# A windowed attention with a ReLU-gated FFN: k and q read row-major and put in order by the PSUM reads, casting loads on the Pool queue, and block 0's denominators in pairs on the ACT queue

## The chip, the cores and the metric

The kernel runs on one core of a Trainium2 chip. The metric is the device time of one execution in microseconds (us). Two runs of the kernel before gave 388.25 and 390.06 us, a median of 389.15 us. The profile is of one further execution.

The engines are named as in the profile: PE is TensorE (matmuls; PEld its weight loads), DVE is VectorE, ACT is ScalarE, POOL is GpSimd, SP is SyncE, which here only issues DMAs. ACT and POOL issue DMAs as well, in their own instruction order; only POOL's can change the data type on the way.

## The reference

Four batches (blocks), eight heads, 768 positions, head size 64; every query sees the first 4 positions (the sink) and the last 128. The attention's output, 3072 tokens of 512, goes through a gated FFN.

```python
scores = scale * np.matmul(q, k.transpose(0, 1, 3, 2))
keep = (pos[None, :] < n_sink) | ((rel >= 0) & (rel < window))      # 4 and 128
scores = np.where(keep, scores, -1000000000.0)
a = np.exp(scores - np.max(scores, axis=-1, keepdims=True))
a = a / (np.sum(a, axis=-1, keepdims=True) + 1e-09)
x = (a @ v) as 3072 x 512
out = (np.maximum(x @ w_gate, 0.0) * (x @ w_val)) @ w_out           # 512 -> 1536 -> 512
```

## The kernel before

Attention is done in units of one block and one pair of heads (`Unit`). Keys are taken in seven windows j of 128 rows, which step by 124; in each window's first four rows stands the sink. A full unit (blocks 1 to 3, twelve of them, `FU`) covers all 768 queries. Block 0 is cut at query 376 (`QCUT`) into four first halves `P0` (windows 0 to 2) and four second halves `P1` (windows 2 to 6), so that the FFN can begin on block 0's first half. Units use two sets of buffers in turn (`s`).

A unit's steps are: `load`, f32 rows of k, q and v by DMA into kf, qf and vf (k and v window by window, 124 rows apart; q row-major, each partition holding n rows in succession); `cast` to bf16 into kn, qn and vn, with copies of the sink rows into windows 1, 3 and 5; `T`, PE transposes of q (L145) and k (L148) into one PSUM tile `tps`, from which DVE copies two halves into qz (L153, L156: the queries, head by head, written in the order of the positions, so with a step of n elements) and ACT copies kT (L154); `S`, score matmuls (L164), the exp on ACT (L167) and the mask product on DVE (L168); `V`, the matmul with v and with a column of ones (L176), which also gives the denominators, copied to oab by ACT (L179).

`norm` takes the denominators through DRAM, since they are to be spread over partitions: row 64 of oab is written to den_tmp (L290), read back as dc (L269), inverted on DVE (L273), written to rcp_tmp (L274), and read as R, broadcast over 64 partitions (L279); then DVE multiplies oab and R into xT (L287). Every step is issued one `tick` after the one before. All of these DMAs stand on SP's queue, as do all loads but the first halves' v.

The FFN runs in chunks (`chunk`): four gate matmuls (L301), the ReLU on ACT (L304), four value matmuls (L307), the product on DVE (L309). There are 96 chunks, 12 for each half block. The output matmuls (L320) of a finished half block are spread between the next chunks.

The order on every engine is that of the program (`manual_schedule`). First the P0 units run by themselves (the prologue), then the stages of P1 and FU are laid between the chunks: two stages to a chunk for the first 18 chunks, then one. A full unit has six stages: T; V of the unit before, with the cast of the next; S of three groups; V of its own first part. Loads are issued three units ahead, casts (on POOL) one unit ahead. The FFN's weights come in by POOL's DMAs, which cast (`load_w`, L184, and `load_wo`, L188).

Of the kernel before, what the change touches and what calls it, by code (L numbers as in the profile page):

```python
# [9 lines left out]
F32 = mybir.dt.float32  # L10
# [11 lines left out]
def kernel(  # L22
# [36 lines left out]
    kf = [const.tile([128, 7, 2, 64], F32, name=f"kf{i}") for i in range(2)]  # L59
    vf = [const.tile([128, 7, 2, 64], F32, name=f"vf{i}") for i in range(2)]  # L60
    qf = [const.tile([128, 6, 2, 64], F32, name=f"qf{i}") for i in range(2)]
    kn = [const.tile([128, 7, 2, 64], BF16, name=f"kn{i}") for i in range(2)]
    vn = [const.tile([128, 7, 2, 128], BF16, name=f"vn{i}") for i in range(2)]
    qn = [const.tile([128, 6, 2, 64], BF16, name=f"qn{i}") for i in range(2)]
    kT = [const.tile([128, 7, 128], BF16, name=f"kT{i}") for i in range(2)]
# [3 lines left out]
    sink = const.tile([4, 2, NP, 2, 64], BF16, name="sink")  # L69
# [5 lines left out]

    class Unit:


        def __init__(self, i, b, p, half):
            self.i, self.b, self.p, self.half, self.s = i, b, p, half, i % 2  # L80
            if half == 0:
                self.js, self.q0, self.n, self.qn, sub = (0, 1, 2), 0, QCUT, 3, p // 2
                self.jo, self.qo, self.zo = 3 * sub, 3 * sub, 384 * sub
                self.qrows, self.qp = 384, 128
            elif half == 1:
                self.js, self.q0, self.n, self.qn = (2, 3, 4, 5, 6), QCUT, S - QCUT, 4
                self.jo, self.qo, self.zo = 0, 0, 0
                self.qrows, self.qp = S - QCUT, 98
            else:
                self.js, self.q0, self.n, self.qn = tuple(range(7)), 0, S, 6  # L90
                self.jo, self.qo, self.zo = 0, 0, 0
                self.qrows, self.qp = S, 128
            self.j5 = [j for j in self.js if j < 6]
            self.a, self.e = self.jo + self.j5[0], self.jo + self.j5[-1] + 1


        def load(self, eng=None, veng=None):
            eng, veng = eng or nc.sync, veng or eng or nc.sync
            s, a, e = self.s, self.a, self.e
            for en, x, dst in ((eng, k, kf[s]), (eng, q, qf[s]), (veng, v, vf[s])):  # L100
                for h in range(2):
                    src = x[self.b, 2 * self.p + h]
                    if x is q:
                        r = src[self.q0:self.q0 + self.qrows, :].rearrange("(p n) d -> p n d", n=self.qn)
                        en.dma_start(out=dst[0:self.qp, self.qo:self.qo + self.qn, h, :], in_=r)
                        continue
                    r = bass.AP(src.tensor, src.offset + 124 * self.j5[0] * D,
                                [[D, 128], [124 * D, e - a], [1, D]])
                    en.dma_start(out=dst[:, a:e, h, :], in_=r)  # L109
                if x is not q and 6 in self.js:  # L110
                    en.dma_start(out=dst[0:24, 6, :, :],  # L111
                                 in_=x[self.b, 2 * self.p:2 * self.p + 2, 744:768, :].rearrange("h s d -> s h d"))


        def cast(self, what, eng):
            s, a, e = self.s, self.a, self.e
            cp = eng.tensor_copy
            if what == "q":
                cp(qn[s][0:self.qp, self.qo:self.qo + self.qn, :, :].rearrange("p j h d -> p (j h d)"),  # L119
                   qf[s][0:self.qp, self.qo:self.qo + self.qn, :, :].rearrange("p j h d -> p (j h d)"))  # L120
                return
            w = 0 if what == "k" else 1
            src, dst = (kf[s], kn[s]) if w == 0 else (vf[s], vn[s])
# [204 lines left out]
    with tc.manual_schedule():  # L328
# [5 lines left out]
        for u in P0:  # L334
            u.load(nc.sync, nc.scalar)
# [172 lines left out]
```

## Time and profile before

| | |
|---|---|
| runs, median | 389.15 us (388.25 to 390.06) |
| profiled execution | 390.11 us, span 388.4 us |
| mean granted PE clock | 0.946 |
| busy, share of the span | PE 70%, DVE 53%, ACT 36%, POOL 21% |
| first FFN matmul that has all of its inputs | 82 us |
| qz copies on DVE (L153, L156), all | 79.8 us of 207.7 us busy |
| DMA | 37.74 MB, 85692 of 96241 packets under 512 bytes |

Busy shares are averages over stages with different limits: the prologue to 82 us, in which PE is mostly idle, the attention units between the chunks to about 318 us, and chunks alone behind that.

### The profile page before, as it was taken

What the parts mean: (1) busy time and instruction counts of PE and PEld (TensorE: products, weight loads), DVE (VectorE), ACT (ScalarE), POOL (GpSimd) and SP (SyncE); (2) the same over time, 40 slices, a digit from 0 to 9 for tenths busy, and PEclk for the clock granted to TensorE, in tenths of its full rate; (3) what the DMA queues carried; (4) which work ended last, traced back from release to release, by engine and by line L of the source; (5) the groups of instructions that cost most, each with busy time, mean ns of one, the idle gap of its engine ahead of it and who ended that gap; (6) DMA issues with size and microseconds to landing.
All of it is one profiled execution on the core that took longest, in us unless ns stands there. A gap on an engine that the chain in (4) does not pass through costs nothing.

```text
span 388.4 us, 5029 instructions
## 1 busy us (share of the span) xinstructions
PE 272.5 (70%) x1760; PEld 163.6 (42%) x1760; DVE 207.7 (53%) x286; ACT 141.3 (36%) x225; POOL 83.2 (21%) x203
## 2 busy tenths in 40 slices
PE   0245230176384695687498989898988999999996
PEld 0122120045252453444255555454645555555552
DVE  5661230347877767861847575767667544222220
ACT  1233120126343543531353544445363533333331
POOL 6240531307424304311404040404010000000000
PEclk9999999999887878969599999999999999999999
DMA  9957199565684554408074747291211211110002
GB/s 178 146 112 125 37 177 196 121 157 117 131 157 102 124 125 94 119 27 166 1 138 95 137 101 137 59 191 33 68 29 43 71 43 53 39 44 29 27 34 103
DMA packets 96241, 37.74 MB, mean 97 GB/s; under 512 B 85692, under 2 KB 92364, under 8 KB 96216
## 3 DMA queue, kind: packets, MB, share of 16 engines
q1 hardware_dynamic: 87208, 31.91, 37.5%
q0 software_dynamic: 5808, 4.72, 8.0%
q10 hardware_dynamic: 3200, 0.79, 1.0%
q8 instruction: 14, 0.23, 0.3%
q14 instruction: 11, 0.09, 0.1%
HBM read 35.64 MB, written 6.49 MB: 108 GB/s over the span
## 4 chain that ended last, share of the span: by engine, by line
PE 48%; DVE 24%; DMA 11%; ACT 6%; issue 4%; SPq 4%; POOL 1%; DVEq 0%; ACTq 0%; POOLq 0%
PE vp L307 14%; PE op L320 13%; PE gp L301 12%; DVE qz L153 10%; DVE qz L156 8%; PE sps L164 6%; DMA kf<-in_k_dram 4%; ACT kT L154 3%; DMA R<-rcp_tmp 3%; DMA dc<-den_tmp 2%; DVE xT L287 2%; PE ops L176 2%; ACT ee L167 2%; SPq L109 2%; SPq L111 1%
## 5 line engine op out<-in xcount | busy, mean ns | idle before, releaser
L307 PE MATMUL vp<-xT,wv 128*128 128x384 bf16 (+2 forms) x384 | 83.2, 342 | 14.2 <-ACT gs L304 14.2
L301 PE MATMUL gp<-xT,wg 128*128 128x384 bf16 (+2 forms) x384 | 84.9, 346 | 5.9 <-DVE hT L309 4.1
L320 PE MATMUL op<-wo,hT 128*128 128x512 bf16 x288 | 77.3, 384 | 0.0
L309 DVE TENSOR_TENSOR hT<-gs,vp 128x384 bf16<-128x384 f32 (+2 forms) x96 | 51.2, 547 | 43.4 <-PE vp L307 42.4
L164 PE MATMUL sps<-qz,kT 128*128 128x251 bf16 (+5 forms) x232 | 35.3, 293 | 47.8 <-DVE qz L156 39.5
L167 ACT ACTIVATE ee<-sps 128x1006 bf16<-128x1006 f32 (+4 forms) x52 | 46.1, 900 | 53.2 <-PE sps L164 53.2
L304 ACT ACTIVATE gs<-gp 128x384 f32<-128x384 f32 (+2 forms) x96 | 47.2, 492 | 41.4 <-PE gp L301 40.9
L307 PEld LDWEIGHTS <-wv 128*128 128x128 bf16 x384 | 39.2, 102 | 47.6 <-issue 25.9
L168 DVE TENSOR_TENSOR ee<-ee,msk 128x1006 bf16<-128x1006 bf16 (+4 forms) x52 | 33.8, 651 | 39.4 <-ACT ee L167 38.8
L287 DVE TENSOR_TENSOR xT<-oab,R 64x768 bf16<-64x768 f32 (+2 forms) x40 | 33.2, 830 | 34.4 <-DMA R<-rcp_tmp 34.1
L128 POOL CAST vn<-vf 128x768 bf16<-128x768 f32 (+2 forms) x20 | 14.7, 732 | 165.8 <-PE ops L176 163.1
L154 ACT COPY kT<-tps 128x896 bf16<-128x896 bf16 (+2 forms) x20 | 15.6, 778 | 95.1 <-DVE qz L153 95.1
L164 PEld LDWEIGHTS <-kT 128*128 128x128 bf16 x232 | 23.0, 113 | 63.6 <-issue 31.9
L156 DVE COPY qz<-tps 64x768 bf16<-64x768 bf16 (+2 forms) x20 | 40.0, 2000 | 17.1 <-ACT kT L154 17.1
L301 PEld LDWEIGHTS <-wg 128*128 128x128 bf16 x384 | 37.3, 103 | 27.6 <-issue 7.9
L176 PE MATMUL ops<-ee,vn 128*128 128x248 bf16 (+6 forms) x256 | 28.6, 255 | 25.8 <-DVE ee L168 18.1
L153 DVE COPY qz<-tps 64x768 bf16<-64x768 bf16 (+2 forms) x20 | 39.8, 1990 | 7.3 <-PE tps L148 7.2
L320 PEld LDWEIGHTS <-hT 128*128 128x128 bf16 x288 | 28.5, 99 | 25.9 <-issue 1.2
L176 PEld LDWEIGHTS <-vn 128*128 128x128 bf16 x256 | 22.5, 103 | 35.0 <-issue 26.5
L179 ACT COPY oab<-ops 65x752 f32<-65x752 f32 (+1 forms) x32 | 25.4, 795 | 25.5 <-PE ops L176 25.3
L145 PE MATMUL tps<-ident,qn 128*128 128x128 bf16 (+1 forms) x100 | 9.8, 236 | 18.5 <-DVE qn L119 18.3
L324 ACT COPY ot<-op 128x512 f32<-128x512 f32 x24 | 14.1, 587 | 22.2 <-PE op L320 22.2
(47 smaller groups left out, 117.9 us busy)
## 6 DMA issues: line engine op xcount, KB each, us to landing
out_dram<-ot SPq DMA_DIRECT2D x24, 256.0 KB
kf<-in_k_dram SPq DMA_DIRECT2D x24, 192.0 KB
qf<-in_q_dram SPq DMA_DIRECT2D x24, 192.0 KB
vf<-in_v_dram SPq DMA_DIRECT2D x24, 192.0 KB
R<-rcp_tmp SPq DMA_DIRECT2D x12, 384.0 KB
wg<-in_moe_w_gate_dram POOLq DMA_DIRECT2D x4, 384.0 KB, 6.3
wv<-in_moe_w_val_dram POOLq DMA_DIRECT2D x4, 384.0 KB, 8.1
wo<-in_moe_w_out_dram POOLq DMA_DIRECT2D x3, 512.0 KB, 16.3
```

The lines of the kernel that those rows point to most:

```text
L153: nc.vector.tensor_copy(zq[0], po[0:64])
L156: nc.vector.tensor_copy(zq[1], po[64:128])
L164: nc.tensor.matmul(out=ps[:, h, c0:c1], lhsT=kT[s][:, self.jo + j, :], rhs=qz[s][:, h, self.zo + q0:self.zo + q0 + c1 - c0], start=True, s ...
L167: nc.scalar.activation(x, ps[:, :, lo:hi], Act.Exp, bias=0.0, scale=scale)
L168: nc.vector.tensor_tensor(x, x, msk[:, gi, :, lo:hi], op=Alu.mult)
L176: nc.tensor.matmul(out=ps[:, h, o0:o0 + c1 - c0], lhsT=vn[s][:, self.jo + j, h, :], rhs=ee[s][:, gi, h, c0:c1], start=i == 0, stop=i == le ...
L287: nc.vector.tensor_tensor(x[64 * h:64 * h + 64, p, q0:q0 + n], oab[0:64, h, q0:q0 + n], R[0][:, h, 0:n], op=Alu.mult)
L301: nc.tensor.matmul(out=gp[:, 0:n], lhsT=wg[:, ko, m * 128:(m + 1) * 128], rhs=x[:, ko, c0:c0 + n], start=ko == 0, stop=ko == KO - 1)
L304: nc.scalar.activation(gs[:, 0:n], gp[:, 0:n], Act.Relu, bias=0.0, scale=1.0)
L307: nc.tensor.matmul(out=vp[:, 0:n], lhsT=wv[:, ko, m * 128:(m + 1) * 128], rhs=x[:, ko, c0:c0 + n], start=ko == 0, stop=ko == KO - 1)
L309: nc.vector.tensor_tensor(hT[:, m, c0:c0 + n], gs[:, 0:n], vp[:, 0:n], op=Alu.mult)
L320: nc.tensor.matmul(out=op, lhsT=hTs[b][:, m, t * 128:(t + 1) * 128], rhs=wo[:, m, :], start=m == 0, stop=m == FM - 1)
```

## The change

*Row-major k.* k is loaded as q is: each partition holds n rows in succession, n being 3 for a first half, 5 for a second and 6 for a full unit. The transposes leave the positions out of order in PSUM. kT (now 872 columns in the order of positions, the last 104 zero) is written in order by an ACT copy that reads PSUM with a step; so are the two halves of qz by DVE, where before PSUM was read in order and qz written with a step. k and q have a PSUM tile each, `tk` and `tq`; the first halves take them from the pool of the FFN. Even windows are now slices of kT; for the odd ones DVE copies 124 columns and the four sink columns into kTs.

*Full units' loads.* They go by POOL's DMAs, which cast from f32 into kn, qn and vn, with no staging and no casts; they are issued in the stage in which the unit before that one ends, one unit ahead. POOL still copies the sink rows of v (`sinkv`).

*Block 0's first denominators.* Each unit writes its own row of den_tmp; the other steps of the chain are made for two units at a time. All of it is issued from ACT's queue. One of the three ticks of each P0 unit is gone.

*Order of the setup.* The buffers' memsets come first; the mask copies on DVE are put behind the first T, and the later masks behind P1's load. P1[3]'s load is issued with P1[2]'s, and `load_wo` behind P1[0]'s T.

```diff
-                    r = bass.AP(src.tensor, src.offset + 124 * self.j5[0] * D,
-                                [[D, 128], [124 * D, e - a], [1, D]])
-                    en.dma_start(out=dst[:, a:e, h, :], in_=r)
+        def load(self, eng, veng, staged):
+            for en, x, dst, r0, pp, nn in ((eng, k, kf[s] if staged else kn[s], self.kr, self.kp, self.kn),
+                                           (eng, q, qf[s] if staged else qn[s], self.qr, self.qp, self.qn)):
+                for h in range(2):
+                    en.dma_start(out=dst[0:pp, self.no:self.no + nn, h, :],
+                                 in_=x[b, 2 * p + h, r0:r0 + pp * nn, :].rearrange("(p n) d -> p n d", n=nn))
+            dst, o = (vf[s], self.vi) if staged else (vn[s], self.vo)
...
+        def sinkv(self, eng):
+            s, odd = self.s, [j for j in self.js if j % 2]
+            src = vn[s][0:4, self.vo, :, 0:64] if self.half != 1 else vsink[:, self.p, :, :]
+            eng.tensor_copy(vn[s][0:4, self.vo + odd[0]:self.vo + odd[-1] + 1:2, :, 0:64], bc(src, len(odd)))
...
-            zq = [qz[s][64 * h:64 * h + 64, h, z0:z0 + w].rearrange("d (p n) -> d n p", n=nq) for h in range(2)]
-            nc.vector.tensor_copy(zq[0], po[0:64])
-            nc.scalar.copy(kT[s][:, self.jo + d0:self.jo + d1, :].rearrange("p j n -> p (j n)"),
-                           ps[:, 1, d0 * 128:d1 * 128])
-            nc.vector.tensor_copy(zq[1], po[64:128])
+            ps = ptile("tk")
...
+            nc.scalar.copy(kT[s][:, k0:k0 + kp * kn_].rearrange("d (p n) -> d p n", n=kn_),
+                           ps[:, 0:kp * kn_].rearrange("d (n p) -> d p n", n=kn_))
+            pq = ptile("tq")
...
+            for h in range(2):
+                r = slice(64 * h, 64 * h + 64)
+                nc.vector.tensor_copy(qz[s][r, h, z0:z0 + qp * qn_].rearrange("d (p n) -> d p n", n=qn_),
+                                      pq[r, 0:qp * qn_].rearrange("d (n p) -> d p n", n=qn_))
+            odd = [j for j in self.js if j % 2]
+            i0, c0 = (odd[0] // 2 + self.no // 3), self.zo + 124 * odd[0] + 4
+            a = kT[s][:, c0:c0 + 124]
+            nc.vector.tensor_copy(kTs[s][:, i0:i0 + len(odd), 4:128],
+                                  bass.AP(a.tensor, a.offset, [a.ap[0], [248, len(odd)], [1, 124]]))
...
+            nc.vector.tensor_copy(kTs[s][:, i0:i0 + len(odd), 0:4], bc(src, len(odd)))
+
+        def kw(self, j):
+            if j % 2:
+                return kTs[self.s][:, j // 2 + self.no // 3, :]
+            c = self.zo + 124 * j
+            return kT[self.s][:, c:c + 128]
...
-    def norm(b, p, oab, q0, n, d):
+    def norm(b, ps, oabs, q0, n, d, eng, first=True, ticks=after):
...
+            eng.dma_start(out=dc[0:pp, 0:g, 0:cc], in_=view(den_d))
...
+            for p in ps:
+                R.append(rpool.tile([64, 2, S], F32, name="R"))
+                eng.dma_start(out=R[-1][:, :, 0:n],
+                              in_=rcp_d[b, p, 2 * q0:2 * (q0 + n)].rearrange("(h s) -> h s", h=2).partition_broadcast(64))
...
         def V0(p):
-            o = new_oab()
-            P0[p].V(0, o)
-            norm(0, p, o, 0, QCUT, 1)
+            o0.append(new_oab())
+            P0[p].V(0, o0[p])
+            den(0, p, o0[p], 0, QCUT, nc.scalar)
+            if p % 2:
+                norm(0, (p - 1, p), o0[p - 1:p + 1], 0, QCUT, 1, nc.scalar)
...
+        P0[0].T(*GV)
+        setup_m0()
...
             P0[p].S("G0")
-            tick()
             P0[p].S("G1a")
...
+                    nxt = at(x + 1)
+                    if nxt is not None:
+                        if nxt.half == 1:
+                            if x >= 1:
+                                casts(nxt)
+                        else:
+                            nxt.load(nc.gpsimd, nc.gpsimd, False)
```

Three places show how rows move. On DVE, the T of the first full unit, before:

```order
L153 COPY qz_99<-tps 64x6x128
L156 COPY qz_99<-tps 64x6x128
L287 TENSOR_TENSOR xT<-oab_105,R 64x392 x2
L273 RECIPROCAL dr<-dc 98x8
L309 TENSOR_TENSOR hT<-gs,vp 128x376
```

and in the change:

```order
L173 COPY qz_101<-tq 64x768 x2
L178 COPY kTs_99<-kT_97 128x3x124
L183 COPY kTs_99<-kT_97 128x3x4
L330 TENSOR_TENSOR xT<-oab_107,R 64x392 x2
L313 RECIPROCAL dr<-dc 98x8
L354 TENSOR_TENSOR hT<-gs,vp 128x376
```

Two copies have come in, the second and third row; the rest stands as it did.

On SP, the den chain of block 0's third and fourth unit (oab_106 and oab_103) and P1[2]'s load, before:

```order
L290 DMA den_tmp<-oab_106 2x1x376
L269 DMA dc<-den_tmp 94x8
L290 DMA den_tmp<-oab_103 2x1x376
L109 DMA kf_85<-in_k_dram 128x4x64 x2
L111 DMA kf_85<-in_k_dram 24x2x64
L105 DMA qf_89<-in_q_dram 98x4x64 x2
L109 DMA vf_87<-in_v_dram 128x4x64 x2
L111 DMA vf_87<-in_v_dram 24x2x64
L274 DMA rcp_tmp<-dr 94x8
L269 DMA dc<-den_tmp 94x8
L279 DMA R<-rcp_tmp 64x2x376
```

and the same chain in the change, on ACT (oab_108 and oab_105 are the third and fourth unit):

```order
L314 DMA rcp_tmp<-dr 94x2x8
L212 COPY oab_108<-ops 65x2x376
L335 DMA den_tmp<-oab_108 2x1x376
L320 DMA R<-rcp_tmp 64x2x376 x2
L212 COPY oab_105<-ops 65x2x376
L335 DMA den_tmp<-oab_105 2x1x376
L164 COPY kT_97<-tk 128x520
L309 DMA dc<-den_tmp 94x2x8
L200 ACTIVATE ee_103<-sps 128x2x375
L314 DMA rcp_tmp<-dr 94x2x8
L200 ACTIVATE ee_103<-sps 128x2x415
L320 DMA R<-rcp_tmp 64x2x376 x2
```

No load stands between the steps any more; what stands there is ACT's own work on P1[0] (kT_97 and ee_103).

On POOL, what a full unit has before:

```order
L125 CAST kn_91<-kf_85 128x768
L130 CAST kn_91<-kf_85 24x128
L135 CAST kn_91<-kf_85 4x128 x3
L119 CAST qn_95<-qf_89 128x768
L128 CAST vn_93<-vf_87 128x12x64
L130 CAST vn_93<-vf_87 24x2x64
L135 CAST vn_93<-vf_87 4x2x64 x3
```

and in the change:

```order
L116 DMA kn_91<-in_k_dram 128x6x64 x2
L116 DMA qn_95<-in_q_dram 128x6x64 x2
L122 DMA vn_93<-in_v_dram 128x6x64 x2
L125 DMA vn_93<-in_v_dram 24x2x64
L149 COPY vn_93<-vn_93 4x3x2x64
```

The casts have become seven DMAs, and one copy is left, behind which the next unit's DMAs stand.

More of the change, by code (lines that the diff above doesn't have):

```diff
@@ L382 @@
         V0(NP - 1)
-        casts(P1[1], nc.gpsimd)
-        P1[2].load()
+        casts(P1[1])
+        P1[2].load(nc.sync, nc.sync, True)
+        P1[3].load(nc.sync, nc.sync, True)
         for c in (2, 3):
             load_w(c)
-        for c in range(3):
-            load_wo(c)
         stages = []
-        rest = P1 + FU
         opart = {}
@@ L413, in first @@
                     newx(u.b)
-                u.T()
+                u.T(*AT)
+                if u.half is None:
+                    u.sinkv(nc.gpsimd)
+                if x == 0:
+                    for c in range(3):
+                        load_wo(c)
             yield first
```

223 lines of the change are left out of this document (112 added, 111 removed).

## The prediction

> **What bounds the kernel now.** I read the page first, then busy time by stretch, then the chain in order of time.
>
> ```profile
> span 388.4 us, 5029 instructions
> PE 48%; DVE 24%; DMA 11%; ACT 6%; issue 4%; SPq 4%; POOL 1%; DVEq 0%; ACTq 0%; POOLq 0%
> ```
>
> Half of the chain that ends last is not TensorE. Where, the stretches tell (TensorE busy, then VectorE; near the end of a row the granted clock and the DMA share):
>
> ```profile
> 0.00:82.00 82.00, 19.92 (x118) 13.18 (x119) 30.04 (x73) 15.83 (x23) 27.52 (x67) 1.00 0.76 133
> 100.00:163.00 63.00, 41.18 (x288) 26.83 (x287) 46.96 (x49) 26.39 (x37) 18.79 (x46) 0.81 0.60 126
> 318.00:388.40 70.40, 66.25 (x366) 35.51 (x363) 18.45 (x32) 21.20 (x41) 0.00 (x0) 0.99 0.13 47
> ```
>
> For 82 us almost nothing runs on TensorE; the last 70 us are full. Between them the attention units set the pace. In the chain a full unit looks so:
>
> ```profile
> 100.19 2.63 DVE qz L153
> 102.84 0.92 ACT kT L154
> 103.78 2.72 DVE qz L156
> 106.63 1.00 PE sps L164 x4
> ...
> 159.58 2.73 DVE qz L153
> ...
> 186.83 2.63 DVE qz L153
> ...
> 296.35 2.63 DVE qz L153
> ```
>
> From the end of the transposes to the first score matmul pass 106.63 - 100.19 = 6.4 us, three copies in a row. The first four units follow each other at (159.58 - 100.19)/4 = 14.8 us, one takes 27.2, the next six 18.3 each, and behind the last T come 388.4 - 296.35 = 92 us.
>
> **The change, part by part.** The prices of the copies:
>
> ```profile
> L156 DVE COPY qz<-tps 64x768 bf16<-64x768 bf16 x12 | 32.7, 2724 | 11.7 <-ACT kT L154 11.7
> L153 DVE COPY qz<-tps 64x384 bf16<-64x384 bf16 x4 | 3.2, 792 | 3.7 <-PE tps L148 3.7
> L309 DVE TENSOR_TENSOR hT<-gs,vp 128x392 bf16<-128x392 f32 x12 | 6.5, 552 | 1.0 <-PE vp L307 0.7
> L309 DVE TENSOR_TENSOR hT<-gs,vp 128x376 bf16<-128x376 f32 x12 | 6.4, 535 | 1.7 <-PE vp L307 1.5
> L218 DVE COPY msk<-msk 128x499 bf16<-128x499 bf16 x1 | 0.3, 293 | 0.0
> L221 DVE COPY msk<-msk 128x20 bf16<-128x20 bf16 x1 | 0.2, 169 | 0.0
> ```
>
> *The copies out of PSUM.* Today each reads PSUM in order and writes qz with a step of 12 bytes (six rows), or 6 bytes (three rows): 2724/768 = 3.5 ns an element against 792/384 = 2.1. The price grows with the step of the write. The change writes in order and reads PSUM with a step of 256 bytes; no row has that. Bounds: an in-order write from PSUM on VectorE, by the two hT rows (17 ns for 16 elements, 1.06 ns each), 552 + 376 x 1.06 = 0.95 us; and 2.72 us if the step costs the same on the reading side. I take 0.95, since the growth goes with the write's step and the hT rows show PSUM reads at one element per cycle.
>
> The Trainium skill speaks against this (PSUM — Partial Sum Buffer, Specifications): PSUM's lines are 8 bytes, and a pattern that isn't contiguous slows matmuls significantly. Were that so for VectorE's reads, the copy would stay at 2.7 us, which is the first rival below; no row here decides it.
>
> New on VectorE are kTs (372 elements, at most the 0.29 of the 499 row) and the sink columns (0.17). kT's own copy on ScalarE no longer waits for the first qz half and runs beside the q transposes. T also takes two PSUM tiles of a ring of two now, so that the V part behind it waits for the kT copy: at most that copy's 0.92 less the q transposes that run meanwhile, half a microsecond, in the early units only; I leave it inside the rounding. So T to score: 2 x 0.95 + 0.29 + 0.17 + 0.2 for handoffs = 2.6 us, 3.8 less than 6.4.
>
> What TensorE itself waits for that copy, first in 100 to 160 us, then in 205 to 296:
>
> ```profile
> PE sps L164 <- DVE qz L156: 19.4, 4, 5.7
> ...
> PE vp L307 <- ACT gs L304: 6.6, 9, 1.0
> PE sps L164 <- DVE qz L156: 4.2, 5, 0.9
> ```
>
> Early units: 4.85 us of wait each, of which 3.8 go; and TensorE at clock 0.81 for 41.2 us loses about 0.19 x 41.2 = 8 us, 1.8 a unit, because the gaps let its clock fall; I take back 0.8. So 4.6 x 4 = 18.4 us; 14.8 becomes 10.2. Late units have two chunks between T and score, which hide most of the copy: 4.2/5 = 0.84 of wait, and 6.6/5 = 1.3 for gs, which stands behind the kT copy on ScalarE half of the time: 1.5 x 7 = 10.5 us. The four half units from 82 to 100 us give 2.
>
> *The long unit.* At 159.58 to 186.83 VectorE waits for R:
>
> ```profile
> 183.72 2.51 DVE L287 TENSOR_TENSOR xT<-oab,R 64x768 bf16<-64x768 f32 x2 [6.93 <-DMA R<-rcp_tmp]
> ...
> 178.83 0.48 SPq L279 DMA_DIRECT2D R<-rcp_tmp  x1
> ```
>
> R is issued behind seven load DMAs on SP. These leave SP altogether, so 6.9 goes, plus 4.6 as above: 11.5.
>
> *The loads as casting DMAs.* A unit has 6 x 768 + 48 = 4656 rows, 291 per DMA engine. Loads now (q1, 100 to 160 us, 256-byte packets nearly all) and casting weight DMAs (q0, 47 to 70 us, packets of 1.5 and 2 KB):
>
> ```profile
> q1 hardware_dynamic: 26034, 7.48, 60.0%
> ...
> q0 software_dynamic: 3693, 3.15, 87.4%
> ...
> L184 POOL DMA_DIRECT2D wg<-in_moe_w_gate_dram x4 | 3.1, 782 | 0.0
> ```
>
> 0.600 x 60 x 16/26034 = 22 ns and 0.874 x 23 x 16/3693 = 87 ns a packet. So a unit's load takes 291 x 22 = 6.4 us, or 25 us if a casting descriptor costs 87 whatever its size. I take about 30 ns, 9 us, near q1, for q0's packets are six to eight times as long. Pool's issue, seven at 0.8 to 1.2 us, fits beside. What hides it: k and q of the next unit are issued once the sink copy of this unit is through, nearly a period ahead. On Pool the sink copy waits for the v that has landed, and the next unit's DMAs stand behind it; if the v is late, so are they, and this is what the third rival is about. The casts removed from Pool were covered by the same lead, worth nothing. `load_wo` keeps its place in Pool's queue (behind the last wg and wv), and P1[3]'s load only moves up on SP, ahead of the half units' den chain.
>
> *The prologue.* The first link of today's den chain, and its end:
>
> ```profile
> 33.35 2.43 DMA den_tmp<-oab
> 35.79 1.52 DMA dc<-den_tmp
> 37.57 1.60 DMA rcp_tmp<-dr
> 39.18 3.45 DMA R<-rcp_tmp
> ...
> 65.40 5.40 DMA dc<-den_tmp
> ...
> 77.32 3.48 DMA R<-rcp_tmp
> ...
> 81.98 0.47 PE gp L301
> ```
>
> On SP the third and fourth pair stand behind P1[2]'s and P1[3]'s loads, whose issue itself stalls while the weights come in; on VectorE a mask product waits behind xT:
>
> ```profile
> 50.11 1.06 SPq L109 DMA_DIRECT2D kf<-in_k_dram  x2
> ...
> 55.27 6.44 SPq L109 DMA_DIRECT2D vf<-in_v_dram  x2
> 61.81 3.17 SPq L111 DMA_DIRECT2D vf<-in_v_dram  x1
> ...
> 10.51 0.29 DVE L125 CAST kn<-kf 128x384 bf16<-128x384 f32 x1
> ...
> 26.84 0.79 DVE L153 COPY qz<-tps 64x384 bf16<-64x384 bf16 x1 [0.92 <-PE tps L148]
> ...
> 42.66 1.10 DVE L287 TENSOR_TENSOR xT<-oab,R 64x376 bf16<-64x376 f32 x2 [4.96 <-DMA R<-rcp_tmp]
> 43.79 0.69 DVE L168 TENSOR_TENSOR ee<-ee,msk 128x1006 bf16<-128x1006 bf16 x1
> ```
>
> The mask copies move behind the first T, so the cast at 10.51 comes some 4 us earlier and P0[3]'s copy at 22 instead of 26.84. In the new order no xT stands ahead of P0[3]'s masks; they end near 30, not 44. Then V0(3), 2 us, a chain of 2.4 + 1.5 + 0.2 + 1.6 + 3.45 = 9.2, two xT of 1.1: 43.5. Against that: on ScalarE, in order, the second pair's DMAs now wait between kT and the exps of P1[0], and share eight completion counters with SP, so that R waits for P1[3]'s first loads to land beside the weights; I put 13.5 on it (two hops at 5.4 instead of 1.5 are 8 of them). The first gp at 57, between 43.5 and 82: 25 us gained.
>
> The skill's rule against this part (DMA: Bandwidth & Descriptors, Issuing engines are not separate DMA queues): all queues run on the same 16 engines, and another issuer saves only issue time. The trace agrees as far as it goes: what I count is SP's issue time (6.44 and 3.17 us for three DMAs), and no hop is counted shorter.
>
> Sum: 25 + 2 + 18.4 + 11.5 + 10.5 = 67.4 from the profiled execution's 390.1 (span 388.4 and 1.7 around it), which is 1 us above the median: 322.7, so 322.
>
> **The rivals.**
>
> *Strided reads as dear as strided writes.* For it speaks that the write's price grows with its step; against it the even PSUM reads. Then T gains 0.5 us for the kT copy alone: 25 + 4 x 0.5 + 8 + 1 = 36, 354 us.
>
> *The prologue stays.* ScalarE waits in order at the den DMAs, and the loads on SP that they wait for come in beside the weights, as P1[2]'s do today. Then 5 instead of 25: 343 us.
>
> *Slower: casting loads set the period.* Place: T of each full unit waits for its load. With period p, T(x4) at 100.2 - 27 = 73, eleven periods and 90 behind: 73 + 11p + 90. It reaches 388 at p = 20.5; less 2.5 for issue and receipt that don't overlap, 18 us over 291 packets is 62 ns. At q0's 87: p = 27.8, 470 us. For it: those are the only casting DMAs in the trace. Against: they are bound by bytes (1.5 to 2 KB in 87 ns). At 50 ns, p = 17, still 352.
>
> **How the numbers follow.** The forecast 0.52, with its own range 305 to 340 (prologue 48 to 66, early units 9 to 12); strided reads 0.14; prologue stays 0.14; loads of 35 to 60 ns, 0.07; slower 0.07; better than 305, 0.06. Taking in the second and third case gives 300 to 358. About 2% is what a measurement tells from no change. Faster by more: all but slower and a strip of the loads between 57 and 65 ns: 0.90; same 0.03; slower 0.07.
>
> **What would show it.** Copies of qz with 768 elements near 0.95 us (wrong at 2 or more); first gp near 57; T to T near 10 us early and 16.8 late; TensorE's wait for qz below 1 us a unit, its clock above 0.9 from 60 to 130 us. A wait of TensorE's transposes for the DMA of kn or qn over 2 us a unit says that the loads bind; ScalarE idle before den DMAs for more than 15 us says that the prologue was mis-sized.

## The result, and the profile after

Two runs of the changed kernel gave 335.64 and 338.31 us, a median of 336.98 us: 0.866 of the time before, with a 95% interval of 0.849 to 0.883. Six more runs of the same kernel, beside the last group of experiments, gave a median of 340.99 us (338.09 to 343.18) and a ratio of 0.8715 (0.8676 to 0.8754). Both are well below 0.98, inside the predicted range of 300 to 358, and 15 to 19 us above the forecast of 322. The profiled execution is the 335.64 one, the fastest of the eight; its span is 333.9 us. The ratios leave out runs that lie over 1.5% above the fastest of their kernel, while the medians take in all runs, so the two can differ a little.

The copies out of PSUM in the changed kernel, VectorE's and ScalarE's (groups by shape: busy time, mean ns of one, idle time before them):

```profile
L173 DVE COPY qz<-tq 64x768 bf16<-64x768 bf16 x24 | 22.9, 953 | 2.9 <-PE tq L168 2.5
```

```profile
L164 ACT COPY kT<-tk 128x768 bf16<-128x768 bf16 x12 | 9.6, 798 | 6.6 <-PE tk L161 6.6
```

The qz copy costs 0.953 us where it cost 2.72: the lower of the two bounds, to the hundredth. The two new kTs copies on VectorE cost 0.33 and 0.18 us.

The stretches (TensorE busy, then its weight loads, VectorE, ScalarE, Pool; then the granted clock, the DMA share and GB/s):

```profile
0.00:69.60 69.60, 19.71 (x119) 12.82 (x120) 29.18 (x82) 15.78 (x23) 24.24 (x52) 0.69 0.87 157
69.60:85.00 15.40, 13.57 (x117) 9.63 (x116) 9.47 (x24) 9.43 (x15) 6.64 (x10) 0.84 0.68 54
85.00:145.00 60.00, 47.52 (x371) 31.82 (x374) 38.67 (x69) 33.61 (x49) 34.20 (x45) 0.97 1.03 97
145.00:260.00 115.00, 106.50 (x747) 66.43 (x759) 67.45 (x115) 60.00 (x96) 32.73 (x44) 1.00 0.64 82
```

From 145 us on TensorE is busy for 93% of the time at full clock; there is little left to gain there. The prologue still takes 69.6 us, with 20 us of TensorE's work in it. Its chain of waits, and then the first FFN matmul that has all of its inputs:

```profile
38.77 6.38 DMA den_tmp<-oab
45.23 13.64 DMA dc<-den_tmp
59.17 3.99 DMA rcp_tmp<-dr
63.23 3.59 DMA R<-rcp_tmp
```

```profile
69.12 0.47 PE L346 MATMUL gp<-xT,wg 128*128 128x376 bf16 x1 [0.66 <-DVE xT L330]
```

The first four rows are the four hops of the second pair's denominators: 27.6 us. Next the transposes of the first, the second, the fifth and the sixth full unit and of the last, by the copies behind them on VectorE:

```profile
84.90 1.93 DVE L173 COPY qz<-tq 64x768 bf16<-64x768 bf16 x2
...
99.14 1.94 DVE L173 COPY qz<-tq 64x768 bf16<-64x768 bf16 x2
...
130.48 1.94 DVE L173 COPY qz<-tq 64x768 bf16<-64x768 bf16 x2 [0.89 <-PE tq L168]
...
148.36 1.94 DVE L173 COPY qz<-tq 64x768 bf16<-64x768 bf16 x2
...
244.66 1.93 DVE L173 COPY qz<-tq 64x768 bf16<-64x768 bf16 x2
```

These five rows give a decomposition of the whole span, which I use for the kernels below (T is a unit's transposes; its place is that of the copy behind them). The differences in the last line add up to the difference of the spans, 54.5 us.

| kernel (profiled execution) | first T of a full unit | four early units | long unit | six late units | behind the last T | span |
|---|---|---|---|---|---|---|
| before | 100.2 | 59.4 | 27.3 | 109.5 | 92.0 | 388.4 |
| changed | 84.9 | 45.6 | 17.9 | 96.3 | 89.2 | 333.9 |
| gained | 15.3 | 13.8 | 9.4 | 13.2 | 2.8 | 54.5 |

### The profile page after: what moved, and what is told of

It is laid out like the page before. It is cut to its first block, busy times and chain, and to the rows that moved or that the text cites. A ratio compares the mean times of both kernels' runs of the same rounds, so it can differ in the third digit from the quotient of the medians.

```text
span 333.9 us, 4812 instructions
## 1 busy us (share of the span) xinstructions
PE 256.6 (77%) x1724; PEld 158.1 (47%) x1748; DVE 164.5 (49%) x323; ACT 140.5 (42%) x225; POOL 97.8 (29%) x151
## 3 DMA queue, kind: packets, MB, share of 16 engines
q1 hardware_dynamic: 27760, 16.62, 19.3%
## 4 chain that ended last, share of the span: by engine, by line
PE 57%; DMA 26%; DVE 6%; issue 4%; ACT 4%; SPq 1%; ACTq 0%; DVEq 0%
PE op L365 16%; PE vp L352 16%; PE gp L346 15%; DMA R<-rcp_tmp 8%; DMA dc<-den_tmp 5%; DMA rcp_tmp<-dr 5%; PE ops L209 4%; DMA den_tmp<-oab 4%; PE sps L197 4%; DMA qf<-in_q_dram 3%; DVE xT L330 2%; ACT oab L212 1%; DVE qz L173 1%; PE tq L168 1%; SPq L116 1%
## 5 line engine op out<-in xcount | busy, mean ns | idle before, releaser
L352 PE MATMUL vp<-xT,wv 128*128 128x384 bf16 (+2 forms) x384 | 79.6, 330 | 5.3 <-ACT gs L349 5.3
L346 PE MATMUL gp<-xT,wg 128*128 128x384 bf16 (+2 forms) x384 | 80.3, 331 | 3.8 <-DVE hT L354 2.9
L365 PE MATMUL op<-wo,hT 128*128 128x512 bf16 x264 | 70.9, 379 | 1.2
L352 PEld LDWEIGHTS <-wv 128*128 128x128 bf16 x384 | 38.0, 99 | 33.8 <-issue 10.2
L173 DVE COPY qz<-tq 64x768 bf16<-64x768 bf16 (+2 forms) x40 | 31.8, 795 | 10.9 <-PE tq L168 10.3
L122 POOL DMA_DIRECT2D vn<-in_v_dram x24 | 19.8, 830 | 58.7 <-issue 57.8
L197 PE MATMUL sps<-qz,kT 128*128 128x251 bf16 (+3 forms) x136 | 28.1, 264 | 8.3 <-DVE qz L173 5.4
L209 PEld LDWEIGHTS <-vn 128*128 128x128 bf16 x256 | 22.5, 103 | 19.8 <-issue 10.7
L197 PE MATMUL sps<-qz,kTs 128*128 128x248 bf16 (+1 forms) x96 | 24.3, 278 | 4.5 <-DVE kTs L183 4.4
L168 PE MATMUL tq<-ident,qn 128*128 128x128 bf16 (+1 forms) x100 | 9.8, 235 | 22.1 <-ACT ee L200 15.2
L161 PE MATMUL tk<-ident,kn 128*128 128x128 bf16 (+1 forms) x104 | 10.1, 237 | 17.1 <-DVE kn L134 13.4
L164 ACT COPY kT<-tk 128x768 bf16<-128x768 bf16 (+2 forms) x20 | 13.9, 693 | 18.1 <-PE tk L161 13.2
```

The costliest lines, as they stand in the source:

```text
L173: nc.vector.tensor_copy(qz[s][r, h, z0:z0 + qp * qn_].rearrange("d (p n) -> d p n", n=qn_), pq[r, 0:qp * qn_].rearrange("d (n p) -> d p n" ...
L197: nc.tensor.matmul(out=ps[:, h, c0:c1], lhsT=self.kw(j), rhs=qz[s][:, h, self.zo + q0:self.zo + q0 + c1 - c0], start=True, stop=True)
L209: nc.tensor.matmul(out=ps[:, h, o0:o0 + c1 - c0], lhsT=vn[s][:, self.vo + j, h, :], rhs=ee[s][:, gi, h, c0:c1], start=i == 0, stop=i == le ...
L346: nc.tensor.matmul(out=gp[:, 0:n], lhsT=wg[:, ko, m * 128:(m + 1) * 128], rhs=x[:, ko, c0:c0 + n], start=ko == 0, stop=ko == KO - 1)
L352: nc.tensor.matmul(out=vp[:, 0:n], lhsT=wv[:, ko, m * 128:(m + 1) * 128], rhs=x[:, ko, c0:c0 + n], start=ko == 0, stop=ko == KO - 1)
L365: nc.tensor.matmul(out=op, lhsT=hTs[b][:, m, t * 128:(t + 1) * 128], rhs=wo[:, m, :], start=m == 0, stop=m == FM - 1)
```

## The experiments

Ratios and medians are given against runs of the kernel before on the same chip (medians 390.1 to 391.2 us). For differences from the changed kernel I take its ratio of six runs, 0.8715; 0.01 is 3.9 us. The table at the end of this section has the decompositions, but for the kernel with wo behind the units. It also has that of the changed kernel's longest execution, 343.18 us: the same kernel, and its columns differ by 0.8 to 2.4 us from those of the 335.64 one. Differences of that size between two rows are not readings.

**The read order undone.**

```diff
-                nc.vector.tensor_copy(qz[s][r, h, z0:z0 + qp * qn_].rearrange("d (p n) -> d p n", n=qn_),
-                                      pq[r, 0:qp * qn_].rearrange("d (n p) -> d p n", n=qn_))
+                nc.vector.tensor_copy(qz[s][r, h, z0:z0 + qp * qn_].rearrange("d (p n) -> d n p", n=qn_),
+                                      pq[r, 0:qp * qn_].rearrange("d (n p) -> d n p", n=qn_))
```

> The changed kernel with one part undone: the two halves of qz read PSUM in order and write qz with the old step; everything else stays. Theory (the step belongs to the write): the 768-element copy goes from 0.953 back to about 2.72 us. A T then takes 3.5 us longer to the first score matmul; the early full units lose about that each (4 x 3.5 = 14), the long one 3.5, the six late ones at most what their cover leaves, 0.8 each, so about 5, and the half units 1: some 24 us, about 361. The prediction's own sum with dear copies was 354, 32 over its forecast, because it gave the clock back as well: that would be 369. Rival (the copies are hidden behind the chunks now that TensorE is over 90% busy from 145 us on): at most the early units show it, under 15 us, 350 or less.

Measured: 366.41 us (364.25 to 369.5), ratio 0.9401 (0.9337 to 0.9466). That is 27 us above the changed kernel. The copy by shape in this kernel:

```profile
L173 DVE COPY qz<-tq 64x768 bf16<-64x768 bf16 x24 | 65.2, 2715 | 4.0 <-PE tq L168 3.6
L173 DVE COPY qz<-tq 64x392 bf16<-64x392 bf16 x8 | 8.2, 1026 | 5.2 <-PE tq L168 5.1
L173 DVE COPY qz<-tq 64x384 bf16<-64x384 bf16 x8 | 6.4, 797 | 2.6 <-PE tq L168 2.5
```

The theory holds as to the price, and the total lies between its two sums (24 and 32). Its places were off: the early units lose 10.4 us rather than 14, the late ones 14.7 rather than 5. So the rival that the copies are hidden in the late units falls. What TensorE waits for there, from 145 to 290 us in this kernel and from 145 to 260 in the changed one:

```profile
PE sps L197 <- DVE kTs L183: 10.0, 5, 3.1
PE sps L197 <- DVE qz L173: 5.6, 4, 3.1
```

```profile
PE sps L197 <- DVE kTs L183: 1.9, 2, 1.4
PE sps L197 <- DVE qz L173: 1.0, 1, 1.0
```

15.6 us instead of 2.9: the score matmuls wait for the two copies, and for kTs, which stands behind them on VectorE.

**The read order alone, on the kernel before.** The same two lines in the other direction, everything else as before.

> The kernel before with one part of the change alone: the two halves of qz are written in order and read PSUM with a step. The copy goes from 2.72 to 0.95 us. If the parts add up, what its undoing cost (29 us) is gained here too, minus what only then became free: 360 to 364. If the early units were held by two things at once, the copies and R behind SP's loads (undoing either cost 10 us there, where both together had gained 14), the gain of the copies alone is smaller, 15 to 22 us: 368 to 375. Rival (no gain without the rest): 385 or more.

Measured: 364.87 us (364.63 to 365.19), ratio 0.9347 (0.9314 to 0.9379): 25 us gained by two lines. Made alone and undone, the part is worth nearly the same (25 and 27). The early units, though, gain only 6.0 us here and the late ones 10.4. TensorE's wait for qz in the early units, 19.4 us before, is down to 0.6 us, but VectorE now waits there for R; first the kernel before (100 to 160 us), then this one (97 to 151):

```profile
DVE xT L287 <- DMA R<-rcp_tmp: 0.6, 1, 0.6
```

```profile
DVE xT L288 <- DMA R<-rcp_tmp: 13.1, 5, 3.8
```

So the early units were held by two things, and the second, R, comes out when the first is gone.

**The loads staged again.**

```diff
...
-                        else:
-                            nxt.load(nc.gpsimd, nc.gpsimd, False)
+                    if nxt is not None and x >= 1:
+                        casts(nxt)
...
+                if nxt3 is not None and nxt3.half is None:
+                    nxt3.load(nc.sync, nc.sync, True)
```

> The changed kernel with the full units' loads as before: f32 rows on SP three units ahead, casts on Pool one unit ahead (a seventh slot in vf for it). Theory of the prediction: what the casting loads bought is SP's queue, so R stands behind load DMAs again in the unit in which that bites: 7 us more, about 344, and the early units keep their pace of about 11 us. Rival (the casting loads, at some 31 ns a 256-byte packet against 22, are the dearer way and hold up the early units and the prologue's tail): then this kernel is as fast or faster, 337 or less. Second rival (SP's issue held up far more than one R): 355 or more.

Measured: 353.98 us (352.92 to 355.57), ratio 0.9082 (0.9028 to 0.9135), 14 us above the changed kernel: twice the 7 of the prediction, and between the theory's 344 and the second rival's 355. The four early units lose 10.0 us and the long one 4.5 (8.5 and 2.1 against the changed kernel's longest execution). SP's queue in this kernel, first beside an early unit and then in the long one:

```profile
89.51 1.27 SPq L116 DMA_DIRECT2D kf<-in_k_dram  x2
90.87 1.29 SPq L116 DMA_DIRECT2D qf<-in_q_dram  x2
92.21 1.30 SPq L122 DMA_DIRECT2D vf<-in_v_dram  x2
93.62 0.77 SPq L125 DMA_DIRECT2D vf<-in_v_dram  x1
94.48 0.34 SPq L314 DMA_DIRECT2D rcp_tmp<-dr  x1
```

```profile
153.78 2.96 SPq L122 DMA_DIRECT2D vf<-in_v_dram  x2
...
157.34 0.49 SPq L320 DMA_DIRECT2D R<-rcp_tmp  x1
```

Each load is 5 us of SP's time, and a hop of a den chain stands behind it in every early unit, not just in the long one. VectorE's wait for R, ahead of the copies of the next T, in the four early units of this kernel and of the changed one:

```profile
DVE xT L330 <- DMA R<-rcp_tmp: 12.4, 4, 4.0
```

```profile
DVE xT L330 <- DMA R<-rcp_tmp: 7.1, 4, 3.0
```

That is 5.3 of the 10.0 us. The rest may be TensorE's granted clock, which from 85 to 145 us is 0.86 here and 0.97 in the changed kernel:

```profile
85.00:145.00 60.00, 44.26 (x310) 28.75 (x310) 37.35 (x62) 28.34 (x42) 15.48 (x24) 0.86 0.66 131
```

0.11 of 44.3 us is 4.9. But that the clock cost this time is not shown: the four runs of this kernel have mean granted clocks of 0.896 (the profiled one), 0.965, 0.968 and 0.968, and took 353.9, 355.57, 352.92 and 354.06 us; and the changed kernel's longest execution has 0.91 in this stretch, with early units of 47.1 us. What is shown is that the loads on SP cost the early units 8.5 to 10 us, and that VectorE waits 5.3 us longer for R in them.

**A third of the casting loads left out.** Without v's loads in the full units.

```diff
+            if not staged:
+                return
             dst, o = (vf[s], self.vi) if staged else (vn[s], self.vo)
```

> The changed kernel without the full units' loads of v (their values stay those of block 0's second halves): 1584 of a unit's 4656 rows, a third of the casting loads, are left out. Theory (the loads are hidden: TensorE's transposes wait 1 us in all for kn and qn): T to T in the early units stays at 10 to 10.8 us and in the late ones at 16, the time falls by 2 us at most. Rival (with all queues together over full from 45 to 60 and from 85 to 145 us, by the DMA share of 1.25 and 1.03, it is the DMA engines that set the early pace by way of R): R comes earlier, the four early units take 40 instead of 45.6 us, and the time falls by 4 to 7 us.

Measured: 331.43 us (330.64 to 332.95), ratio 0.8494 (0.846 to 0.8529), 9 us below the changed kernel: more than either theory allowed. The place is neither theory's: in the profiles the early units take 43.9 us (45.6 in the changed kernel), the long one 16.3 (17.9), the late ones 93.1 (96.3), each also below the changed kernel's longest execution. TensorE's transposes never wait long for a load in either kernel, but the loads are not free. Pool's queue in the changed kernel from 85 to 145 us:

```profile
q0 software_dynamic: 25794, 3.22, 85.0%
```

0.850 x 60 x 16/25794 = 31.6 ns for a packet, and all queues together ask for 1.03 of the 16 engines there. The rival's way was R, and in the early units it was not that: without v's loads VectorE waits 6.8 us for R there, with them 7.1. The spans differ by 5.1 us and the medians by 9.6, since the profiled execution of the changed kernel is the fastest of its eight; what part of the gain comes from the relieved DMA engines, and what from Pool's freed queue, stays open.

**The chain on SP, in single units, and the masks first.** Three parts undone one at a time: `den` and `norm` of block 0's first halves with `nc.sync` in the place of `nc.scalar`; one `norm` for each unit instead of one for two; `setup_m0()` and `setup_m1()` ahead of the memsets.

```diff
-            den(0, p, o0[p], 0, QCUT, nc.scalar)
+            den(0, p, o0[p], 0, QCUT, nc.sync)
...
-            if p % 2:
-                norm(0, (p - 1, p), o0[p - 1:p + 1], 0, QCUT, 1, nc.scalar)
+            norm(0, (p,), o0[p:p + 1], 0, QCUT, 1, nc.scalar)
...
         setup_pool()
+        setup_m0()
+        setup_m1()
```

> The changed kernel with block 0's first denominators issued from SP again, still in pairs, in the same order of the program: the second pair's dc stands behind P1[2]'s and P1[3]'s loads there. Theory A (the queue is what counted): the first FFN matmul goes from 69 towards the 82 us of before, 10 us or more lost, about 348. Theory B (the second pair's chain is held by the weights that come in between 38 and 66 us, whatever queue issues it): the first FFN matmul stays within 3 us of 69 and the time within 3 us of 337.

> The changed kernel with the pairing undone: each first half of block 0 has its own dc, reciprocal, rcp and R, still on ACT's queue. It does twice as many hops, of which those of the fourth unit come last beside the weights. If pairing is part of why the first FFN matmul comes at 69 instead of 82 us (the run with the chain on SP left 71.6, so the queue is worth about 2.5 of those 13), it moves to 75 or later and the time to 342 or more. If it is nothing, 337 within 2.

> The changed kernel with the order of the setup undone: all mask copies on VectorE ahead of the memsets and of the first T. The prediction put 4 to 5 us on the earlier first T. Theory: the first T, the first den and the second pair's den come some 4 us later, and the second pair's den then falls wholly into the weights, so the first FFN matmul is 4 us later or more, 341 or above. Rival: the chain's hops are set by the transfers beside them, which end at the same time (66 us) in any case: the first FFN matmul at 69 still, 337 within 2.

Measured: 342.45 us, 0.8763 (0.8706 to 0.882); 342.76 us, 0.874 (0.8681 to 0.8799); 342.12 us, 0.8766 (0.8722 to 0.8811). All three intervals overlap the changed kernel's; the parts come out at 1 to 2 us each, none of them clear of noise. The first FFN matmul that has all of its inputs comes at 71.6, 72.5 and 72.3 us instead of 69.1: 2.5, 3.4 and 3.2 of the 13 us by which it moved. So the queue alone is not what gained the 13 us, nor is the pairing its main cause; added up, the three small things make 9 of the 13, or 6 if they are counted from the longest execution of the changed kernel, in which this matmul comes at 70.1. Where the rest comes from (the tick left out, fewer rows of k, P1[3]'s load or wo moved) was not tried part by part.

With the chain on SP the first pair's rcp takes 10.6 us, and the second pair's hops come late:

```profile
35.15 10.63 DMA rcp_tmp<-dr
...
50.68 6.19 DMA qf<-in_q_dram
...
61.09 2.14 DMA dc<-den_tmp
...
63.52 2.22 DMA rcp_tmp<-dr
65.76 3.54 DMA R<-rcp_tmp
```

That rcp runs beside the weights, whose last packets move before 55 us. SP issues in order: behind that rcp's R come two units' loads, from 47.9 to 61.0 us, and only then dc, which takes 2.1 us. On ACT's queue dc is issued at 45.2 us and takes 13.6. It arrives at 63.2 on SP and at 58.9 on ACT. So the first FFN matmul stays within 3 us, as theory B forecast, but dc itself is not stretched here: what holds it is its place behind the loads, which is theory A's mechanism, and only the hop ahead of them is stretched by the weights. The chain on SP with the weights held back was not tried, so what ACT's queue is worth without the weights stays open.

**The weights behind the chain.**

```diff
-        for c in (2, 3):
-            load_w(c)
...
+        gt = const.tile([1, 1], F32, name="gt")
+        nc.gpsimd.tensor_copy(gt[:], lastR[1][0:1, 0, 0:1])
+        for c in (2, 3):
+            load_w(c)
+        for c in range(3):
+            load_wo(c)
```

`lastR[1]` is R of the second pair; the weights stand behind the copy on Pool, just ahead of the first chunk in the program.

> The changed kernel, with the last two quarters of wg and wv and all of wo held on Pool until the second pair's R has landed (Pool copies one element of R, then issues them). Theory B (those weights stretch the second pair's dc to 13.6 us, den to 6.4 and rcp to 4): dc falls under 4 us, the first FFN matmul comes at about 55 instead of 69; what is gained is partly given back if the weights or the casting loads queued behind them come late: 325 to 332. Rival (dc is held by P1[3]'s loads on SP, which stay where they are, or by the two-way wait on a completion counter): dc stays over 8 us, the first FFN matmul over 64 us, and the time is 337 or more.

Measured: 330.37 us (329.79 to 332.16), ratio 0.8479 (0.8437 to 0.8521), 9 us below the changed kernel. The second pair's hops in this kernel, and what comes later:

```profile
39.25 4.63 DMA den_tmp<-oab
43.96 1.85 DMA dc<-den_tmp
46.11 2.22 DMA rcp_tmp<-dr
...
49.02 3.69 DMA R<-rcp_tmp
...
69.26 7.22 DMA vn<-in_v_dram
```

12.4 us where they took 27.6. P1's loads on SP stay where they were, so it is the weights that stretched dc: this half of theory B is shown. The first FFN matmul with all inputs comes at 54.2 us, earlier than the forecast's 57:

```profile
54.21 0.32 PE L349 MATMUL gp<-xT,wg 128*128 128x376 bf16 x1 [0.81 <-DVE xT L333]
```

But T of the first full unit gains only 8.3 us, since its loads now stand behind wo, and 2.8 of those are lost again behind it. By its interval this kernel is faster than the kernel before and the changed one.

**The weights spread further.** wo's pieces one each behind the loads of the first three full units; then the second quarter of wg and wv behind R as well; and, on the kernel with the weights behind the chain, block 0's k and q laid out so that a partition's rows of one head are one piece.

```diff
                             nxt.load(nc.gpsimd, nc.gpsimd, False)
+                            if x <= 5:
+                                load_wo(x - 3)
...
-        for c in (2, 3):
+        for c in (1, 2, 3):
             load_w(c)
...
-    kf = [const.tile([128, 6, 2, 64], F32, name=f"kf{i}") for i in range(2)]
+    kf = [const.tile([128, 2, 6, 64], F32, name=f"kf{i}") for i in range(2)]
```

> The kernel with the last quarters of wg and wv behind the second pair's R, and wo's three pieces issued one each behind the loads of the first three full units (they were all ahead of them). In the run before this the first FFN matmul came at 54, but TensorE's first full-unit T waited for kn and qn that stood behind wo, and only 8 of the 15 us were left at that T. Theory: the wait goes, T of the first full unit comes at about 70, and the time is 323 to 327. Rival (what is given back lies in the R waits of the half units and in TensorE's own work): 329 or more.

> As the kernel with wo behind the units, and the second quarter of wg and wv also held until the second pair's R. Theory: the hops of the chain between 22 and 48 us (den 5.2 and 4.6 us where 1.5 was seen at 22 us) are stretched by that quarter, and by P1's loads; without it the first FFN matmul comes at 47 to 50, and the time is 3 or 4 us below the kernel with wo behind the units. Rival (P1's loads alone stretch them, or the quarter then arrives too late for chunk 3): no gain, or up to 3 us slower.

> The kernel with the weights behind the second pair's chain, and kf and qf laid out head by head, so that a partition's 3, 4 or 5 rows of one head are one piece of 768 to 1280 bytes for block 0's loads; the cast puts them in the old order. In the trace of the changed kernel the first two qf waits of the chain are 4.0 and 6.5 us, and den takes 5 us beside P1's loads. Theory (these are packets of 256 bytes at some 22 ns on all engines, 13,400 of them, 18 us of 16 engines): both waits and den shrink, the first FFN matmul comes 3 to 5 us before 54, and 2 to 4 us are left at the end: 326 to 329. Rival (bytes, not packets, set these loads): 330 within 1.

Measured: 334.67 us, 0.8492 (0.8433 to 0.855); 333.61 us, 0.8555 (0.8497 to 0.8612); 333.59 us, 0.8536 (0.85 to 0.8572). None is faster than the kernel with the weights behind the chain, and the three theories fall. In the second of them, which has the first one's edit as well, the first full unit's T comes 4.3 us earlier than in the kernel with the weights behind the chain, at 72.3, and the four early units take 51.5 us instead of 45.6. VectorE waits for R there:

```profile
78.69 1.13 DVE L333 TENSOR_TENSOR xT<-oab,R 64x392 bf16<-64x392 f32 x2 [3.75 <-DMA R<-rcp_tmp]
...
87.92 1.13 DVE L333 TENSOR_TENSOR xT<-oab,R 64x392 bf16<-64x392 f32 x2 [5.14 <-DMA R<-rcp_tmp]
```

The weights have to come in somewhere before 100 us; moved off one chain of denominators, they seem to stretch the next one. In the third, q1 has 17984 packets instead of 27760, and the first FFN matmul is still at 54.3 us: the number of q1's packets is not what sets it.

**The changed kernel once more**, beside the last three of these.

> The changed kernel as it is, timed in five rounds beside the three below, since its time above rests on two runs. Expected 337 within 1.5, and above the kernel with the weights behind the chain (330.4) by 5 to 7 us.

Measured: 340.99 us, as told at the start, outside the 337 within 1.5; the kernel with the weights behind the chain is 0.024 of the time before below it, 9 us, and the intervals do not meet.

| kernel (profiled execution) | first T of a full unit | four early units | long unit | six late units | behind the last T | span |
|---|---|---|---|---|---|---|
| changed, longest execution | 86.0 | 47.1 | 20.3 | 98.0 | 90.0 | 341.4 |
| read order undone | 85.9 | 56.0 | 20.9 | 111.0 | 91.6 | 365.3 |
| read order alone | 97.3 | 53.4 | 24.2 | 99.1 | 89.3 | 363.4 |
| loads staged | 85.7 | 55.6 | 22.4 | 97.4 | 91.2 | 352.2 |
| chain on SP | 87.0 | 45.2 | 19.7 | 97.5 | 89.4 | 338.7 |
| single chains | 87.5 | 47.1 | 19.9 | 97.8 | 89.4 | 341.7 |
| masks first | 86.9 | 45.1 | 20.8 | 98.1 | 90.0 | 340.9 |
| no v loads | 84.9 | 43.9 | 16.3 | 93.1 | 90.6 | 328.8 |
| weights behind chain | 76.6 | 45.6 | 18.7 | 97.5 | 90.0 | 328.4 |
| a quarter more behind | 72.3 | 51.5 | 20.5 | 99.4 | 89.1 | 332.8 |
| weights behind, wide rows | 77.4 | 46.2 | 19.8 | 99.9 | 89.5 | 332.8 |

## Why the prediction was right, and where it was off

The forecast took 67.4 us from the profiled execution; 54.5 went. By its own steps:

*The copies out of PSUM.* Right. 0.95 was chosen over 2.72 because the price grew with the step of the write and not of the read, and 0.953 was measured; ScalarE's kT copy now reads with the same step and takes 798 ns for 768 elements; read in order, in the kernel before, it took 480 ns for 384, 692 for 640 and 906 for 896, and the line through these gives 799 for 768. From T to the last of the copies that the scores wait for pass 2.7 us (148.36 to 151.08, rows of the long unit below) where 2.6 were forecast. The rule of the Trainium skill (PSUM — Partial Sum Buffer, Specifications), of which the first rival was made, is not borne out by these reads of VectorE and ScalarE; it speaks of matmuls, which no run here has with such a pattern. Between its two cases the prediction had 32 us; 25 and 27 were measured.

*Early units, 14.8 to 10.2.* They follow each other at 14.2, 10.0, 10.6 and 10.8 us; three of the four are as forecast. In the first, two den chains of the half units come late; R holds VectorE, and behind it the copies of the next T:

```profile
90.01 1.13 DVE L330 TENSOR_TENSOR xT<-oab,R 64x392 bf16<-64x392 f32 x2 [2.78 <-DMA R<-rcp_tmp]
...
97.44 1.13 DVE L330 TENSOR_TENSOR xT<-oab,R 64x392 bf16<-64x392 f32 x2 [3.04 <-DMA R<-rcp_tmp]
```

The step that failed is the division of the gain: all 18.4 us were put on the copies and the clock, and the loads on SP were counted in the long unit alone. Copies alone gain 6.0 there, with VectorE then waiting 13.1 us for R; staging the loads costs 10.0. That 13.8 of the 18.4 us came all the same is in part luck: the change removed the second cause too, for which the prediction had nothing in this term. Of its signs for these stages, TensorE's wait for qz is as forecast (3.1 us in four units); its clock from 60 to 130 us is 0.87 and not above 0.9.

*The long unit, 27.2 to 15.7.* 17.9. R no longer stands behind loads. VectorE still waits 5.5 us for it (at 145.94), but TensorE works through most of that; of its idle times between 140 and 152 us the longest are these:

```profile
149.36 0.28 PE L197 MATMUL sps<-qz,kT 128*128 128x255 bf16 x1 [0.99 <-DVE qz L173]
151.08 0.28 PE L197 MATMUL sps<-qz,kTs 128*128 128x248 bf16 x1 [1.43 <-DVE kTs L183]
```

The term took off all of VectorE's 6.9 us of waiting for R and a whole early unit's copy. But what TensorE itself waited for behind that R, in the kernel before, was less:

```profile
186.88 1.47 PE L301 MATMUL gp<-xT,wg 128*128 128x392 bf16 x4 [4.06 <-DVE hT L309]
```

With its 4.1 us of wait for qz in this unit that is 8.2 us, and not 11.5; 9.4 were gained. In this unit the program also changes from two stages to a chunk to one: it has six chunks in the changed kernel where the early unit ahead of it has three, so more of it is work that the change leaves alone.

*Late units, 18.3 to 16.8.* 16.05 on average, 13.2 us gained over the six, where 10.5 were counted for seven. Read order alone gave 10.4; the term's size was about right for the copies, and what the rest of the change adds there was not counted.

*The casting loads.* About 30 ns a packet was taken; 31.6 was measured. They do not set the period (the slower rival falls: the period is 10 to 11 us in the early units, and no wait of TensorE for a DMA is among its groups of waits), but the sentence that 9 us of load lie hidden is right only in part: a third of them costs 9 us of time.

*The prologue, 82 to 57.* This is the step that was mis-sized: 69.1 us, so 13 gained and not 25. ScalarE's waits from 20 to 70 us were the sign named for it:

```profile
ACT ee L200 <- DVE dr L313: 13.1, 1, 13.1
ACT ee L200 <- DMA den_tmp<-oab: 5.5, 1, 5.5
ACT ee L200 <- DMA vf<-in_v_dram: 5.1, 1, 5.1
```

These are 23.7 us, above the 15 named. The prediction gave 9.2 us for the chain and 13.5 for what stands against it, with two hops at 5.4, and let R wait for P1[3]'s loads. R waited for nothing but rcp (rcp landed at 63.16, R was issued at 63.23). Measured were hops of 6.4, 13.6, 4.0 and 3.6, since the last two quarters of the weights and wo are issued from 37.6 us on, just ahead of the second pair's denominators:

```profile
37.58 0.75 POOL L217 DMA_DIRECT2D wg<-in_moe_w_gate_dram  x1
...
40.50 2.26 POOL L221 DMA_DIRECT2D wo<-in_moe_w_out_dram  x3
...
45.23 0.24 ACTq L309 DMA_DIRECT2D dc<-den_tmp  x1
```

The weights' place on Pool's queue had been read as unchanged. Their order is, but the change issues them 9.6 us earlier (37.6 where it was 47.2), and the chain, earlier as well, now meets them in the middle; with the weights behind the chain the first FFN matmul comes at 54.2. The rule that was cited for this part (the Trainium skill, DMA: Bandwidth & Descriptors, Issuing engines are not separate DMA queues) says that another issuer saves only the time of issuing. By the sum the trace with the chain on SP agrees, 71.6 us against 69.1; by its hops it says less, since dc there stood behind 13 us of SP's issuing. Holding the weights back moves the first FFN matmul by 14.9 us, more than the 12 that were missed, but of the time only 5.5 us in the span and 9 by the ratios; the rest is lost again to loads behind wo and in the units behind.

## What to carry to other kernels

Where a copy has to reorder, put the step on the PSUM side: here a step of 256 bytes on the read cost nothing that can be measured (953 ns against 950 estimated from the in-order rows on VectorE, 798 against 799 on ScalarE), and one of 12 bytes on the SBUF write cost 2.3 ns an element more than writing in order. When a chain of small DMAs is moved earlier, look at which bulk transfers it will then run beside, and hold those back with a real dependency rather than by their place in a queue; then ask which chain they will meet next. A part's share of a gain is found by undoing it and by making it alone: here, of five parts undone one by one, one carried half of the gain and three could not be told from noise.

## What the runs showed of the hardware that was not expected

A read of 6 KB (94 rows of two pieces of 32 bytes) took 1.85 us in the kernel with the weights held back and 2.1 in the one with the chain on SP, with other loads beside it (91 and 110 GB/s on all queues meanwhile), and 13.6 us beside the weights of another queue (195 GB/s). R, 376 KB in two DMAs, took 3.6 us in that same kernel at 63 us and 3.7 in the one with the weights held back. The Trainium skill (DMA: Bandwidth & Descriptors, Why a DMA increments its semaphore by 16 and not by 1) states that a DMA is spread over the largest number of engines up to 16 that divides the slowest dimension of both its source and its destination; for 94 rows on both sides that would be, by estimate, two engines. No run here shows which engines carried it, and a chain with 96 rows was not tried.

The step of the write has its own price list, from the kernel with the read order undone: 797/384 = 2.1 ns an element at 6 bytes, 1026/392 = 2.6 at 8, 2715/768 = 3.5 at 12. The same copies written in order, in the changed kernel, are 555/384 = 1.4, 563/392 = 1.4 and 953/768 = 1.2 (what an instruction costs is in all of them).

Casting packets on Pool's queue (256 bytes read, 128 written) took 31.6 ns where SP's of 256 bytes took 22 in the kernel before, and still the kernel with them is 14 us faster than the one with the loads staged, at a DMA share of 1.03 against 0.66 from 85 to 145 us: what they relieve is a queue, not the engines.
